# A kernel's first 30 microseconds: W_in in four equal parts behind x, halos on VectorE, a different order for W_out

## The chip, the cores and the metric

The kernel runs on one core of one Trainium2 chip. The metric is the device time of one execution in microseconds (us). A profile's own span is some 1.5 to 2 us shorter than the time of its execution, so spans are compared only with spans, and times only with times. One profile of each kernel is kept. That of the kernel before fell in a run of 683.38 us, which only one of its 34 other runs on record beats; against its span, a difference therefore comes out some 0.5 us larger than the same difference of the times. "Clock" is the mean clock that was granted to TensorE over an execution, with 1.000 as the full one.

## The reference, cut to what matters

```python
# x: (8, 4096, 192) float32; weight: (8, 7); w_in: (192, 2048); w_out: (2048, 192)
w = softmax(weight, axis=-1)                    # 8 heads, 7 taps
x_pad = concatenate([zeros((8, 6, 192)), x], axis=1)
x_unf = x_pad[:, idx, :].reshape(8, 4096, 7, 8, 24)
x = einsum('hk,bskhg->bshg', w, x_unf)          # causal convolution along s, weights shared in a head
h = x.reshape(32768, 192) @ w_in
g = 0.5 * h * (1.0 + erf(h / sqrt(2)))          # exact Gelu
out = g @ w_out
```

## The kernel before

The 32,768 tokens are worked off in blocks. A block takes `w` tokens from each of two halves of the token range, one half on partitions 0 to 63, the other on 64 to 127, and the 192 channels as three planes of 64. Blocks 0 and 1 have 256 tokens in each half, and TensorE computes their convolution with seven diagonal weight matrices (`dg`). From block 2 on VectorE computes it. Then TensorE multiplies by W_in, ScalarE takes the Gelu, and TensorE multiplies by W_out.

Everything that the change touches belongs to the start. GpSimd issues W_in, builds the identity matrix, and then does the halos of block 0 (the tokens just ahead of each strip of 32) and the casts of block 1:

```python
        @block.gpsimd
        def _(g):
            # win_in(c0, c1, sm): two transfers, one for each half of W_in's columns
            win_in(FP[0], FP[1], S_WIN[0])          # FP = [0, F/8, 2F/8, F/2]
            # ... wait for the memset, build the identity idb ...
            for i in range(1, 3):
                win_in(FP[i], FP[i + 1], S_WIN[i])  # part 2 is twice as large
            # ...
            g.wait_ge(S_IDN, 2)
            halo(0)      # zeros, then one copy a plane, each after its transpose
            halo(1)
            for p in range(NP):
                cast(g, 1, p)
            # ... casts of W_out, further halos ...
```

The queue of SP carries x and W_out. It waits once, for the first part of W_in, and the rest goes in one order:

```python
        @block.sync
        def _(sp):
            sp.dma_start(wsb[:, :], ...).then_inc(S_WSB, 16)   # the convolution's weights
            load(sp, 0, (0, 1))                     # half of block 0's x; ScalarE issues the other
            sp.wait_ge(S_WIN[0], 32)
            load(sp, 1)
            # ... four transfers of W_out, 384 KB each ...
            load(sp, 2)
            load(sp, 3)
```

VectorE prepares the weights, then transposes, copies and duplicates W_in, so that both halves of the partitions have all of it. TensorE begins with matmuls on zeros, the warm-up; in the profile of before their weight loads come 0.43 us apart up to 4.21 us, and then eight in 1.61 us:

```python
            for p in range(NP):                     # VectorE
                trans(0, p)
            conv_out(v, 0, 1)
            conv_out(v, 0, 4)
            dup(0)
            dup(1)
            for p in range(NP):
                trans(1, p)
            dup(2)
            # ...
            for i in range(16):                     # TensorE
                t.matmul(hp[1][:, 0:512], warm[:, 0:128], warm[:, :])
```

## Time and profile before

| | before |
|---|---|
| time, median of 3 | 683.76 us (683.46 to 684.16) |
| span of the profile | 681.6 us |
| TensorE busy | 675.0 us, 99% |
| first Gelu of block 0 | 10.10 us |
| transposes of block 1 | 12.41 us |
| transposes of block 2 | 19.65 us |
| first weight load of block 2 | 29.14 us |

A line of the timeline reads: start in us, how long the group was busy, engine, source line, operation, result and operands with their shapes, number of instructions, and in brackets the idle time of the engine before it and what ended it. A line of busy time by stretch has the stretch, its length, the busy time and number of instructions of TensorE's matmuls (PE), its weight loads (PEld), VectorE (DVE), ScalarE (ACT) and GpSimd (POOL), then the granted clock, the DMA share and the GB/s that the DMA engines moved. A line of waits has: who waited, for what, us in all, how often, the longest.

```profile
1.32 1.40 POOL L384 DMA_DIRECT2D win<-in_moe_w_in_dram  x2 [0.80 <-POOLq L905]
...
13.89 0.96 PE L711 MATMUL ob<-xTb,dg 64*64 64x256 bf16 x28
...
15.65 1.02 ACT L681 ACTIVATE gT<-hp 128x1024 bf16<-128x1024 f32 x1 [0.63 <-PE hp L760]
```

### The profile page before, as it was taken

The page shows a single profiled execution, that of the slowest core. Times are in us where ns is not written, and L with a number is a line of the kernel's source. Part 1 is how long each engine was busy: PE and PEld are TensorE (multiplying, and loading weights), DVE is VectorE, ACT ScalarE, POOL GpSimd, SP SyncE. Part 2 cuts the span into 40 slices and gives each one's busy share as a digit, 9 for nine tenths or more (in the row PEclk, how much of TensorE's full clock was granted, in tenths as well). Part 3 has the DMA queues.
Part 4 walks back from the last instruction along what each step waited for, and adds up shares of the span by engine and source line. Part 5 has one row for each costly group of instructions (what it writes and reads, how often), then busy time and mean ns, then how long its engine had stood idle before and what let it go on. Part 6 is the DMA issues. An engine that isn't in the chain of part 4 may idle for free.

```text
span 681.6 us, 27317 instructions
## 1 busy us (share of the span) xinstructions
PE 675.0 (99%) x12576; PEld 410.1 (60%) x12576; DVE 561.0 (82%) x904; ACT 537.3 (79%) x550; POOL 38.9 (6%) x57
## 2 busy tenths in 40 slices
PE   8999999999999999999999999999999999999998
PEld 4899655555555555555555555555555555555556
DVE  6899979888889888899888898888898888988611
ACT  6899988787787777787777788777878777878772
POOL 5026000000000000000000000000000000000000
PEclk9999999999999999999999999999999999999999
DMA  9446323234332244332244422334322434310123
GB/s 222 86 101 134 79 60 75 43 75 95 96 94 58 45 91 94 95 86 47 60 94 95 94 69 46 78 94 96 94 52 46 95 94 96 83 42 21 48 49 94
DMA packets 132994, 54.79 MB, mean 80 GB/s; under 512 B 126480, under 2 KB 132752, under 8 KB 132880
## 3 DMA queue, kind: packets, MB, share of 16 engines
q1 hardware_dynamic: 130960, 51.50, 32.5%
q8 instruction: 98, 1.61, 1.0%
q0 software_dynamic: 1248, 0.79, 0.9%
q10 hardware_dynamic: 672, 0.76, 0.4%
q14 instruction: 16, 0.13, 0.1%
HBM read 28.66 MB, written 25.17 MB: 79 GB/s over the span
## 4 chain that ended last, share of the span: by engine, by line
PE 96%; ACT 2%; DMA 1%; issue 0%; DVE 0%; SPq 0%; ACTq 0%
PE hp L760 48%; PE ob L824 43%; PE ob L791 6%; ACT gT L681 2%; DMA xin<-in_x_dram 1%; PE ob L711 0%; ACT xc L191 0%; ACT osb L269 0%; DVE osb L311 0%; DVE xT L526 0%; ACT xTb L630 0%; SPq L872 0%; DVE osb L280 0%; SPq L329 0%; ACTq L629 0%
## 5 line engine op out<-in xcount | busy, mean ns | idle before, releaser
L681 ACT ACTIVATE gT<-hp 128x1024 bf16<-128x1024 f32 x512 | 523.3, 1024 | 128.8 <-PE hp L760 125.5
L760 PE MATMUL hp<-xc,win 64*64 64x512 bf16 (+2 forms) x6048 | 419.5, 366 | 1.5 <-ACT gT L681 0.7
L824 PE MATMUL ob<-gT,wout 64*64 64x512 bf16 x5376 | 366.3, 376 | 0.0
L559 DVE SCALAR_TENSOR_TENSOR acc<-xT,wcol,acc 128x512 f32<-128x512 f32 (+1 forms) x495 | 314.1, 698 | 0.0
L760 PEld LDWEIGHTS hp<-xc,win 64*64 64x64 bf16 (+1 forms) x6048 | 189.9, 106 | 134.8 <-ACT gT L681 2.5
L824 PEld LDWEIGHTS ob<-gT,wout 64*64 64x64 bf16 x5376 | 172.3, 118 | 122.8
L311 DVE STREAM_TRANSPOSE osb<-ob 128x512 f32<-128x512 f32 x84 | 74.1, 885 | 100.8 <-PE ob L824 100.8
L526 DVE STREAM_TRANSPOSE xT<-xin 128x512 f32<-128x512 f32 (+1 forms) x105 | 78.6, 797 | 3.8 <-DMA xin<-in_x_dram 3.8
L559 DVE SCALAR_TENSOR_TENSOR xc<-xT,wcol,acc 128x512 bf16<-128x512 f32 (+1 forms) x99 | 65.0, 708 | 0.0
L447 POOL COPY xT<-xT 128x18 f32<-128x18 f32 x30 | 27.9, 930 | 505.2 <-DVE xT L526 482.9
L791 PE MATMUL ob<-wout,gT 64*128 64x192 bf16 x1024 | 52.9, 243 | 0.3
L791 PEld LDWEIGHTS ob<-wout,gT 64*128 64x128 bf16 x1024 | 44.9, 94 | 5.2 <-PE ob L791 0.6
L552 DVE TENSOR_SCALAR acc<-xT,wcol 128x512 f32<-128x512 f32 (+1 forms) x90 | 37.5, 474 | 1.1
L282 ACT ACTIVATE osb<-ob 128x192 f32<-128x192 f32 x4 | 1.3, 332 | 9.5 <-PE ob L791 9.5
L280 DVE COPY osb<-ob 128x192 f32<-128x192 f32 x4 | 1.4, 358 | 8.4 <-PE ob L791 8.4
L695 PE MATMUL hp<-warm 128*128 128x512 bf16 x16 | 5.1, 485 | 1.3 <-DVE warm L463 1.3
L269 ACT ACTIVATE osb<-ob 128x384 f32<-128x384 f32 x12 | 5.8, 486 | 0.0
L654 ACT ACTIVATE acc<-xT,wcol 128x256 f32<-128x256 f32 (+1 forms) x9 | 5.2, 575 | 0.0
L695 PEld LDWEIGHTS hp<-warm 128*128 128x128 bf16 x16 | 1.8, 119 | 4.0 <-issue 1.9
L384 POOL DMA_DIRECT2D win<-in_moe_w_in_dram x6 | 3.9, 658 | 0.8 <-POOLq L905 0.8
L711 PE MATMUL ob<-xTb,dg 64*64 64x256 bf16 (+1 forms) x112 | 3.2, 245 | 0.7 <-ACT xTb L630 0.7
L193 DVE CAST xc<-ob 64x256 bf16<-64x256 f32 (+3 forms) x8 | 2.8, 357 | 1.3 <-PE ob L711 1.1
(31 smaller groups left out, 22.4 us busy)
## 6 DMA issues: line engine op xcount, KB each, us to landing
out_dram<-osb SPq DMA_DIRECT2D x122, 192.0 KB, 3.1
xin<-in_x_dram SPq DMA_DIRECT2D x116, 192.0 KB, 4.1
xin<-in_x_dram SPq DMA_DIRECT2D x20, 96.0 KB, 4.2
woutf<-in_moe_w_out_dram SPq DMA_DIRECT2D x4, 384.0 KB, 6.2
win<-in_moe_w_in_dram POOLq DMA_DIRECT2D x4, 96.0 KB, 4.6
win<-in_moe_w_in_dram POOLq DMA_DIRECT2D x2, 192.0 KB, 5.1
out_dram<-osb SPq DMA_DIRECT2D x8, 48.0 KB, 1.9
out_dram<-osb ACTq DMA_DIRECT2D x4, 96.0 KB, 1.9
```

The lines of the kernel that those rows point to most:

```text
L269: e.activation(out=dst, in_=src, func=AF.Copy).then_inc(S_EVA)
L311: v.transpose(ap(osb[m % 2], j, [[8 * C, 128], [C // 2, TB // 32], [NP, 32]]), bank(ring(m, j)),).then_inc(S_EV)
L447: g.tensor_copy(dst, src).then_inc(S_HALO)
L526: v.transpose(ap(xT[n % 2], p * XW + HX, [[NP * XW, 128], [1, w]]), ap(xin[n % NX], p, [[TB // 32 * DQ, 128], [D if n == 0 else DQ, w // 3 ...
L552: ins = v.tensor_scalar(a, src, wk, None, ALU.mult)
L559: ins = v.scalar_tensor_tensor(dst, src, wk, a, op0=ALU.mult, op1=ALU.add)
L654: a.activation(out=acc[n % 2][:, p * TB : p * TB + w], in_=ap(xT[n % 2], p * XW + HX, [[NP * XW, 128], [1, w]]), func=AF.Copy, scale=wcol[ ...
L681: a.activation(out=ap(gT[n % 2], i * c * 2 * w, dst), in_=ap(hp[u % 2], 0, src), func=AF.Gelu,).then_inc(S_GELU)
L695: t.matmul(hp[1][:, 0:512], warm[:, 0:128], warm[:, :])
L760: ins = t.matmul(hp[u % 2][fo : fo + fw, o : o + w], ap(win, f1, [[NP * F, 64], [2, fw]]), xc[n % 2][r, p * TB : p * TB + w], start=(p == ...
L791: ins = t.matmul(bank(bb[sub], w=C), gT[m % 2][r, c0 : c0 + 128], wout[r, CH[sub][i] * C : (CH[sub][i] + 1) * C], start=(ph == 0 and i == ...
L824: ins = t.matmul(bank(ring(m, j), slice(64 * h, 64 * h + 64), w), ap(wout, 64 * hf * NF * C + CH[h][i] * C + j, [[NF * C, 64], [NP, 64]],) ...
```

## The change

The intent is to let block 0's x move without W_in beside it by making W_in wait, to shrink that x, to take GpSimd out of block 0's path, to let the duplicates of W_in follow smaller parts, and to let the first eight units of block 0's results need only half of W_out.

```diff
             def win_in(i):                        # four parts, F/8 columns of each half, 1 KB rows
-            win_in(FP[0], FP[1], S_WIN[0])        # GpSimd: first of all
-            for i in range(1, 3):
-                win_in(FP[i], FP[i + 1], S_WIN[i])
             g.wait_ge(S_IDN, 2)
             halo(0)                               # now only the zeros
+            g.wait_ge(S_PRO, 1)                   # VectorE has seen the convolution's weights land
+            for i in range(4):
+                win_in(i)
...
-                    src = [[mb * D, 32], [1, mb * D - DQ]]      # block 0's x: long rows, 720 KB
+                    src = [[mb * D, 32], [D, mb], [1, DQ]]      # 384-byte rows, 384 KB
...
             for p in range(NP):                   # VectorE
                 trans(0, p)
+                v.wait_ge(S_TR, p + 1)
+                v.tensor_copy(...).then_inc(S_HALV)             # halo, was GpSimd's
+            v.wait_ge(S_TR, NP)
+            v.tensor_copy(...).then_inc(S_CASTV)                # third cast, was ScalarE's
             conv_out(v, 0, 1)
             conv_out(v, 0, 4)
             dup(0)
             dup(1)
+            dup(2)
             for p in range(NP):
                 trans(1, p)
-            dup(2)
+            dup(3)
...
-            for i in range(16):                   # TensorE: warm-up
+            for i in range(10):
...
-            share = {1: [4, 8, 8, 8, 9, 9, 9, 9]}
+            share = {1: [4, 4, 9, 9, 9, 9, 10, 10]}   # block 0's result units behind each unit of block 1
+                if m == 0:                        # W_out's first half serves both groups first
+                    us.sort(key=lambda q: not (q[1] == 0 and q[2] < 4))
...
-            sp.wait_ge(S_WIN[0], 32)              # SP, ahead of block 1's x
+            sp.wait_ge(S_WIN[1], 32)
```

More of the change, by code (lines that the diff above doesn't have):

```diff
@@ L135, in bass_lightweight_conv__then__act_gelu_exact_kernel @@
         S_WSB = sem("S_WSB")
-        S_WIN = [sem("S_WIN%d" % i) for i in range(3)]
+        S_WIN = [sem("S_WIN%d" % i) for i in range(4)]
         S_WOUT = [sem("S_WOUT%d" % i) for i in range(4)]
@@ L148, in bass_lightweight_conv__then__act_gelu_exact_kernel @@
         S_CAST = [sem("S_CAST%d" % i) for i in range(len(PC))]
+        S_CASTV = sem("S_CASTV")
         S_PC = sem("S_PC")
@@ L153, in bass_lightweight_conv__then__act_gelu_exact_kernel @@
         S_HALO = sem("S_HALO")
+        S_HALV = sem("S_HALV")
         S_TR = sem("S_TR")
@@ L206, in bass_lightweight_conv__then__act_gelu_exact_kernel @@
         FH = F // 2
-        FP = [0, FQ, 2 * FQ, FH]
         WG = [0, 4, 2, 6]
@@ L224, in bass_lightweight_conv__then__act_gelu_exact_kernel @@
         for n in range(NB):
-            HC.append(HC[n] + (1 + NP if n == 0 else 1))
+            HC.append(HC[n] + 1)
         def wcols(hf, f):
@@ L321, in load @@
                 off = ((q // 2) * HALF + OFF[n]) * D + DQ * (q % 2)
+                dst = [[TB // 32 * DQ, 32], [DQ, mb], [1, DQ]]
                 if n == 0:
-                    dst = [[TB // 32 * DQ, 32], [1, mb * D - DQ]]
-                    src = [[mb * D, 32], [1, mb * D - DQ]]
+                    src = [[mb * D, 32], [D, mb], [1, DQ]]
                 else:
-                    dst = [[TB // 32 * DQ, 32], [DQ, mb], [1, DQ]]
                     src = [[D, 32], [32 * D, mb], [1, DQ]]
@@ L381, in _, with win_in @@
         def _(g):
-            def win_in(c0, c1, sm):
+            def win_in(i):
+                c0 = FQ * i
                 for hf in range(2):
                     g.dma_start(
-                        ap(win, 64 * hf * NP * F + c0, [[NP * F, 64], [F, NP], [1, c1 - c0]]),
-                        ap(wint, hf * FH + c0, [[NP * F, 64], [F, NP], [1, c1 - c0]]),
-                    ).then_inc(sm, 16)
-            win_in(FP[0], FP[1], S_WIN[0])
+                        ap(win, 64 * hf * NP * F + c0, [[NP * F, 64], [F, NP], [1, FQ]]),
+                        ap(wint, hf * FH + c0, [[NP * F, 64], [F, NP], [1, FQ]]),
+                    ).then_inc(S_WIN[i], 16)
             g.wait_ge(S_MSET, 1)
@@ L411, in halo @@
                     ).then_inc(S_HALO)
-                    for p in range(NP):
-                        g.wait_ge(S_TR, p + 1)
-                        g.tensor_copy(
-                            ap(t, p * XB + 1, [[NP * XB, 128], [32, HB], [1, 31]]),
-                            ap(
-                                xT[0],
-                                p * XW + HX + WS[0] - HL,
-                                [[NP * XW, 128], [32, HB], [1, 31]],
-                            ),
-                        ).then_inc(S_HALO)
                     return
@@ L504, in dup @@
                             win,
-                            64 * (1 - hf) * NP * F + FH + FP[s],
-                            [[NP * F, 64], [F, NP], [1, FP[s + 1] - FP[s]]],
-                        ),
-                        ap(
-                            win,
-                            64 * hf * NP * F + FP[s],
-                            [[NP * F, 64], [F, NP], [1, FP[s + 1] - FP[s]]],
-                        ),
+                            64 * (1 - hf) * NP * F + FH + FQ * s,
+                            [[NP * F, 64], [F, NP], [1, FQ]],
+                        ),
+                        ap(win, 64 * hf * NP * F + FQ * s, [[NP * F, 64], [F, NP], [1, FQ]]),
                     ).then_inc(S_DUPE)
@@ L525, in trans @@
                         v.wait_ge(S_HALO, HC[n])
+                    if n == 2:
+                        v.wait_ge(S_HALV, NP)
                 v.transpose(
@@ L530, in trans @@
                         p,
-                        [[TB // 32 * DQ, 128], [D if n == 0 else DQ, w // 32], [NP, 32]],
+                        [[TB // 32 * DQ, 128], [DQ, w // 32], [NP, 32]],
                     ),
@@ L581, in _ @@
                 trans(0, p)
+                v.wait_ge(S_TR, p + 1)
+                v.tensor_copy(
+                    ap(xTb[0], p * XB + 1, [[NP * XB, 128], [32, HB], [1, 31]]),
+                    ap(xT[0], p * XW + HX + WS[0] - HL, [[NP * XW, 128], [32, HB], [1, 31]]),
+                ).then_inc(S_HALV)
+            v.wait_ge(S_TR, NP)
+            v.tensor_copy(
+                ap(xTb[0], (NP - 1) * XB + HL, [[NP * XB, 128], [1, WS[0]]]),
+                ap(xT[0], (NP - 1) * XW + HX, [[NP * XW, 128], [1, WS[0]]]),
+            ).then_inc(S_CASTV)
             conv_out(v, 0, 1)
@@ L627, in _ @@
             a.wait_ge(S_PRO, 9)
-            for p in range(NP):
+            for p in range(NP - 1):
                 a.wait_ge(S_TR, p + 1)
@@ L700, in pconv @@
                 if k == KS - 1:
-                    t.wait_ge(S_CAST[PC[n]], p + 1)
+                    if n == 0 and p == NP - 1:
+                        t.wait_ge(S_CASTV, 1)
+                    else:
+                        t.wait_ge(S_CAST[PC[n]], p + 1)
                     if n == 0:
@@ L704, in pconv @@
                 if k == KS - 2:
-                    t.wait_ge(S_HALO, HC[n] + 2 + p if n == 0 else HC[n + 1])
+                    t.wait_ge(S_HALO, HC[n + 1])
+                    if n == 0:
+                        t.wait_ge(S_HALV, p + 1)
                 for hf in range(2):
@@ L743, in mm1 @@
                         t.wait_ge(S_CV, cvd(n))
-                if n == 0 and i < 3:
+                if n == 0 and i < 4:
                     t.wait_ge(S_WIN[i], 32)
-                if n == 0 and 4 <= i < 7:
+                if n == 0 and i >= 4:
                     t.wait_ge(S_DUPE, 2 * (i - 4) + 2)
@@ L844, in units @@
                     return [(ps, i) for ps in range(3) for i in range(NF)]
-                return [
-                    (g, ph, i) for g in range(NG[m]) for ph in range(2) for i in range(NF)
-                ]
+                us = [(g, ph, i) for g in range(NG[m]) for ph in range(2) for i in range(NF)]
+                if m == 0:
+                    us.sort(key=lambda q: not (q[1] == 0 and q[2] < 4))
+                return us
             for n in range(NB):
```

## The prediction

> **What bounds the kernel now.** I read the page first, then busy time by stretch, then the timeline of the first 32 us instruction by instruction, then the waits of the engines and of the DMA queue. The engine totals first:
>
> ```profile
> PE 675.0 (99%) x12576; PEld 410.1 (60%) x12576; DVE 561.0 (82%) x904; ACT 537.3 (79%) x550; POOL 38.9 (6%) x57
> ```
>
> TensorE is busy for 675.0 of 681.6 us, so only 6.6 us of its idle time exist at all. The stretches say where:
>
> ```profile
> 0.00:5.00 5.00, 3.74 (x11) 1.43 (x12) 2.42 (x13) 3.36 (x6) 3.74 (x11) 1.00 0.64 161
> 5.00:10.00 5.00, 3.94 (x77) 2.51 (x76) 3.13 (x9) 2.48 (x7) 2.18 (x7) 1.00 1.23 177
> 10.00:15.00 5.00, 4.24 (x82) 2.81 (x78) 3.34 (x7) 4.88 (x5) 1.99 (x4) 1.00 1.05 323
> 15.00:20.00 5.00, 4.73 (x104) 3.50 (x101) 3.27 (x8) 4.11 (x6) 2.95 (x5) 1.00 1.26 226
> 20.00:25.00 5.00, 4.93 (x108) 4.46 (x104) 4.96 (x15) 3.89 (x4) 0.31 (x1) 1.00 0.31 57
> 30.00:35.00 5.00, 5.00 (x113) 5.00 (x109) 4.96 (x14) 4.37 (x6) 0.31 (x1) 1.00 0.42 98
> ```
>
> (Columns: stretch, length, busy PE, PEld, DVE, ACT, POOL, clock, DMA share, GB/s.) From 30 us TensorE is full. Everything that the diff touches lies before that, so the change can only move the moment at which the full stretch begins. The first stretch also counts the warm-up matmuls as busy, which compute nothing. The timeline of that part:
>
> ```profile
> 4.62 0.63 DVE L491 TENSOR_TENSOR dg<-idb,wcol 128x448 bf16<-128x448 bf16 x1
> 5.93 1.33 DVE L526 STREAM_TRANSPOSE xT<-xin 128x256 f32<-128x256 f32 x3 [0.68 <-DMA xin<-in_x_dram]
> 6.52 1.15 POOL L414 CAST xTb<-xT 128x186 bf16<-128x186 f32 x3 [0.48 <-DVE xT L526]
> 6.55 1.17 ACT L630 ACTIVATE xTb<-xT 128x256 bf16<-128x256 f32 x3 [2.23 <-DVE xT L526]
> 7.02 1.68 PE L711 MATMUL ob<-xTb,dg 64*64 64x256 bf16 x56 [0.71 <-ACT xTb L630]
> 8.01 1.38 ACT L191 ACTIVATE xc<-ob 128x256 bf16<-128x256 f32 x4 [0.30 <-PE ob L711]
> 10.10 4.92 ACT L681 ACTIVATE gT<-hp 128x1024 bf16<-128x1024 f32 x5 [0.71 <-PE hp L760]
> ...
> 13.79 1.99 DVE L502 COPY win<-win 64x1536 bf16<-64x1536 bf16 x2
> ...
> 19.65 1.35 DVE L526 STREAM_TRANSPOSE xT<-xin 128x256 f32<-128x256 f32 x3 [1.54 <-DMA xin<-in_x_dram]
> ...
> 27.77 1.26 DVE L559 SCALAR_TENSOR_TENSOR xc<-xT,wcol,acc 128x256 bf16<-128x256 f32 x3
> ...
> 29.14 0.58 PEld L760 LDWEIGHTS hp<-xc,win 64*128 64x128 bf16 x12 [0.15 <-issue]
> ```
>
> Two paths run from start to 29.14, where block 2's first matmuls begin. **Path A**: x of block 0 lands, is transposed, cast, convolved on TensorE (7.02), copied out, multiplied by W_in, and the first Gelu starts at 10.10. From there eight Gelus of 1.02 us, with block 1's convolution matmuls wedged in, set the pace until block 1 begins at 18.01; then TensorE is full. **Path B**: x of block 2 lands only at 19.65 (VectorE idles 1.54 us for it), and from then VectorE works without a gap until the last result of block 2's convolution, 27.77 + 1.26 = 29.03. TensorE's weight load follows at 29.14 after 0.15 us of idle that the profile calls issue. The preceding weight loads ended at 28.21 + 0.78 = 28.99, so both paths arrive together, B last by about 0.15 us. A gain on A alone is worth at most that 0.15 us unless B moves too.
>
> [...]
> 1. [...] the DMA share is 1.05 to 1.26 from 5 to 20 us, while W_in (GpSimd), x and W_out (SP) are all in flight. [...]
> 2. [...] The trace's bf16 copies fit such a fixed part: 64x768 takes 0.42 us (1.77 for four), 64x1536 takes 0.68, so 0.16 us is left at zero size.
> 3. [...] Here warm-up weight loads come 0.43 us apart up to 4.21 us, then eight in 1.61 us[...].
> 4. [...] This trace shows contention between compute instructions (a GpSimd cast took 0.65 beside a VectorE copy against 0.40 alone; a copy 1.28 against 0.68), but not that W_in's issue suffers from it.
>
> **The change part by part.**
> *x of block 0.* Four loads of 180 KB in long rows become four of 96 KB in 384-byte rows: 720 to 384 KB, and W_in now waits until wsb has landed, so it no longer shares the engines with x. Last landing now is 5.93 minus a few hundredths. With the same issue times (0.88 to 2.05 us) and the quickest landing of such a line at 2.5 us, I estimate 4.5 to 5.0. But VectorE's own program has dg before the transpose, until 4.62 + 0.63 = 5.25. So the transposes start at 5.27, gaining 0.66 and not 1.2 us.
> *Halos and the third cast on VectorE.* GpSimd took 0.38 us a halo, beside the transposes. [...] Each halo also waits for its own transpose (about 0.04 us). Chain from 5.27: transpose to 5.79, halo 6.08, transpose to 6.52, halo 6.81, transpose to 7.25, halo 7.54, cast 7.79. ACT's cast of plane 1 ends at 6.52 + 0.10 + 0.42 = 7.04 (before 7.31), but plane 2 is ready at 7.79 (before 7.72). The 0.66 us is eaten by the serial chain. Convolution starts at 6.36 instead of 7.02, but planes 1 and 2 finish within 0.05 us of before, and ACT's four copies from 8.4 us on then lead to the first Gelu at about 10.03: gain 0.07 us.
> *Ten warm-up matmuls for sixteen.* They end near 4.9 us; [...] Zero.
> *W_in.* Eight issues of 0.63 us (six took 3.93), started at about 2.4 us after the reduce at 2.17, end at 7.6. Parts then land[...] near 6, 7, 8.3 and 9.5 us. Each is wanted at 8.9, 9.9, 11.2 and 12.1 by TensorE, so none delays it. The SP queue now waits for part 1, about 6.9, where it waited for part 0 and resumed at 6.53: block 1's x and W_out are issued 0.4 us later, but meet less W_in, because x's traffic shrank by 336 KB and W_in is no longer queued deep ahead of them.
> *The duplicate copies.* The pair of 0.68 and 1.28 us after block 1's transposes becomes a pair of 0.42 before and a pair after. VectorE is free for block 1's copies at about 14.5, not 15.78; the sixth unit's matmuls (16.06) come about 0.1 us earlier, and Gelu 7 follows. Gain 0.13 us.
> *W_out's order.* The first eight of 64 result units need only half of W_out, whose last cast runs at 18.22 to 19.05. No wait on it is seen now in TensorE's idle, so this is insurance for an earlier start. Work is unchanged: 0.
> *Sum.* Path A: 0.07 + 0.13 = 0.2 us. Path B: block 2's x lands by my estimate about 1 us earlier, since the same queue carries less[...]. Then B has slack and the start of block 2 follows A: the 0.15 us of waiting goes as well. Total 0.35 us: 683.76 - 0.35 = 683.4.
>
> **The rivals.**
> *R1: block 2's x lands later.* SP waits for a later part of W_in; if GpSimd's first bytes take 2.5 us after issue (they came in the packets of before only as x's were ending), part 1 lands at 8 us, everything behind it moves by up to 1.5 us, and path B ends at 29.6 to 30.2. The time becomes 684.4 to 685. For it: B has no slack. Against: x is out of W_in's way.
> *R2: VectorE's serial chain is longer,* [...] With 0.15 us on each of four instructions the first Gelu moves to 10.6: about 684.1. [...]
> *R3: the gain of x passes through whole* (0.66 us, because ACT, not the copies of planes 1 and 2, sets the Gelu) and B moves too: 682.9.
>
> **Range and chances.** The sum gives 683.4. R3 and run-to-run spread (683.46 to 684.16) give the low side, 682.6; R1 and R2 give the high side, 684.4. I put 0.25 on R1 or R2. A change of 2% is 13.7 us, twice all TensorE's idle time, so faster is nearly excluded[...].
>
> **What would show it.** In the timeline after: transposes of block 0 directly behind dg at 5.25 (first step); halo copies of 0.25 us, cast ready near 7.8; convolution at 6.4 with a hole in it; first Gelu near 10.0; block 2's transposes near 18.7 and VectorE done before TensorE needs it at about 28.9. If the transposes of block 2 start after 19.65, R1 holds; if the halos take over 0.35 us, R2; if the first Gelu is before 9.6, R3. A cold clock (warm-up weight loads still 0.43 us apart at the end and slow convolution matmuls) would break the prediction altogether.

(The sum came to 0.35 us, hence 683.4: 0.07 and 0.13 us on path A, and 0.15 us of waiting once path B has slack. The 0.07 comes from the chain of VectorE; for a halo and for the third cast the profile after measured 0.26 and 0.29 us, and 0.03 to 0.04 us from a transpose's end to its halo. The zero for the ten warm-ups rested on a limit for idle time, and the landings of W_in's parts on an allowance after their last issue; neither was shown. Path B's 1 us was the estimate, and no working from measured numbers stands for it.)

## More of the kernel before

```profile
SPq L329 <- DMA win<-in_moe_w_in_dram: 4.5, 1, 4.5
```

GpSimd issues W_in's first part at 1.32 us; block 1's convolution runs at 13.89 us without having waited; the sixth Gelu starts at 15.65.

## The result, and the profile after

The changed kernel took 685.79 us in the median of four runs (684.94 to 687.52); the kernel before, on the same chip in the same rounds, took 683.96 (683.46 to 684.24). The ratio is 1.0031, with a 95% interval of 1.0007 to 1.0054. It is thus slightly slower, well within 2%, and above the predicted range. (All ratios here are the mean time of one kernel's fast runs over that of the other's of the same rounds, so not quite the ratio of the quoted medians.) The four runs fall into two pairs: 684.94 and 684.97 at a clock of 1.000, and 686.61 and 687.52 at 0.998 and 0.997. The profiled run is the 686.61.

The engine totals of the changed kernel, from its page:

```profile
PE 676.4 (99%) x12570; PEld 407.7 (60%) x12570; DVE 561.9 (82%) x910; ACT 537.3 (78%) x549; POOL 38.5 (6%) x56
```

TensorE's busy time grew by 1.4 us with six matmuls fewer; so some of them ran more slowly. Busy time by stretch, changed kernel:

```profile
0.00:5.00 5.00, 3.74 (x9) 1.34 (x10) 2.41 (x13) 3.37 (x6) 3.22 (x11) 1.00 0.46 93
5.00:10.00 5.00, 4.00 (x76) 2.27 (x76) 4.18 (x13) 2.23 (x7) 2.98 (x6) 1.00 1.16 142
10.00:15.00 5.00, 3.02 (x46) 1.74 (x42) 2.24 (x6) 4.83 (x5) 0.12 (x1) 1.00 0.99 285
15.00:20.00 5.00, 4.56 (x80) 3.00 (x82) 3.26 (x9) 1.02 (x1) 4.08 (x7) 0.66 1.17 253
20.00:25.00 5.00, 4.53 (x94) 3.92 (x90) 4.27 (x13) 4.71 (x5) 0.86 (x3) 1.00 0.46 100
```

Three things differ from before. The DMA engines move 93 and 142 GB/s in the first two stretches, where it was 161 and 177. TensorE is busy for 3.02 us from 10 to 15 us instead of 4.24. And from 15 to 20 us the granted clock is 0.66, where it was 1.00 throughout.

The timeline of the changed kernel:

```profile
2.63 5.14 POOL L385 DMA_DIRECT2D win<-in_moe_w_in_dram  x8 [0.51 <-DVE wmx L458]
...
5.17 0.51 DVE L515 STREAM_TRANSPOSE xT<-xin 128x256 f32<-128x256 f32 x1
5.72 0.26 DVE L573 CAST xTb<-xT 128x186 bf16<-128x186 f32 x1
...
6.25 2.34 PE L717 MATMUL ob<-xTb,dg 64*64 64x256 bf16 x56 [0.54 <-ACT xTb L631]
...
9.92 4.93 ACT L682 ACTIVATE gT<-hp 128x1024 bf16<-128x1024 f32 x5 [0.71 <-PE hp L766]
...
14.30 1.32 DVE L515 STREAM_TRANSPOSE xT<-xin 128x256 f32<-128x256 f32 x3 [2.66 <-DMA xin<-in_x_dram]
...
15.34 1.78 PE L717 MATMUL ob<-xTb,dg 64*64 64x256 bf16 x28 [1.55 <-POOL xTb L214]
...
17.05 1.46 PE L766 MATMUL hp<-xc,win 64*128 64x256 bf16 x12
...
18.55 1.02 ACT L682 ACTIVATE gT<-hp 128x1024 bf16<-128x1024 f32 x1 [3.70 <-PE hp L766]
...
21.03 1.34 DVE L515 STREAM_TRANSPOSE xT<-xin 128x256 f32<-128x256 f32 x3 [0.66 <-DMA xin<-in_x_dram]
...
29.14 1.27 DVE L548 SCALAR_TENSOR_TENSOR xc<-xT,wcol,acc 128x256 bf16<-128x256 f32 x3
```

Read it in two halves. Up to 9.92 us everything is as intended: block 0's transposes start 0.76 us earlier, and the first Gelu 0.18 us earlier. After that both later blocks are late. Block 1's x lets its transposes start at 14.30 instead of 12.41 us; TensorE waits 1.55 us for it, and Gelu, which follows, idles 3.70 us. Block 2's x starts its transposes at 21.03 instead of 19.65, and VectorE's chain ends at 29.14 + 1.27 = 30.41 instead of 29.03.

The wait of SP's queue for W_in, changed kernel:

```profile
SPq L328 <- DMA win<-in_moe_w_in_dram: 5.2, 1, 5.2
```

It ends at 7.86 us in the chain of waits, where the queue of before resumed at 6.53.

In this profile block 2's first weight load is at 32.29 us, 3.15 us later than before, and the span grew by 684.8 - 681.6 = 3.2 us. VectorE's chain accounts for 1.4 of them. The other 1.8 belong to TensorE, which was still behind with block 1. The matmuls at 17.05 show why: twelve take 1.46 us, and twelve of the same form took 0.83 at 12.95 us, where the granted clock was 1.00. In stretches of half a microsecond the granted clock is 0.50 from 16.1 to 19.5 us: half of 3.4 us, so by estimate 1.7 us of TensorE's work, are lost there.

### The profile page after: what moved, and what is told of

Read it like the earlier page. It is cut to its first block, busy times and chain, and to the rows that moved or that the text cites. A ratio compares the mean times of both kernels' runs of the same rounds, so it can differ in the third digit from the quotient of the medians.

```text
span 684.8 us, 27315 instructions
## 1 busy us (share of the span) xinstructions
PE 676.4 (99%) x12570; PEld 407.7 (60%) x12570; DVE 561.9 (82%) x910; ACT 537.3 (78%) x549; POOL 38.5 (6%) x56
## 3 DMA queue, kind: packets, MB, share of 16 engines
q8 instruction: 98, 1.61, 1.0%
## 4 chain that ended last, share of the span: by engine, by line
PE 95%; ACT 2%; DMA 1%; POOL 0%; issue 0%; DVE 0%; SPq 0%
PE hp L766 47%; PE ob L830 42%; PE ob L797 5%; ACT gT L682 1%; DMA xin<-in_x_dram 1%; DMA win<-in_moe_w_in_dram 0%; PE ob L717 0%; POOL win L385 0%; DMA wsb<-in_weight_dram 0%; SPq L328 0%; ACT osb L270 0%; DVE osb L312 0%; POOL xTb L214 0%; DVE xT L515 0%; DVE osb L281 0%
## 5 line engine op out<-in xcount | busy, mean ns | idle before, releaser
L766 PEld LDWEIGHTS hp<-xc,win 64*64 64x64 bf16 (+1 forms) x6048 | 187.9, 106 | 136.7 <-ACT gT L682 2.9
L717 PE MATMUL ob<-xTb,dg 64*64 64x256 bf16 (+1 forms) x112 | 4.8, 288 | 2.4 <-POOL xTb L214 1.6
L717 PEld LDWEIGHTS ob<-xTb,dg 64*64 64x64 bf16 x112 | 3.2, 124 | 4.7 <-POOL xTb L214 2.1
```

The lines of the kernel that those rows point to most:

```text
L717: ins = t.matmul(bank(kd, slice(64 * ho, 64 * ho + 64), w), dg[r, d0 : d0 + 64], xTb[PC[n]][r, x0 : x0 + w], start=(k == KS - 1), stop=(k ...
L766: ins = t.matmul(hp[u % 2][fo : fo + fw, o : o + w], ap(win, f1, [[NP * F, 64], [2, fw]]), xc[n % 2][r, p * TB : p * TB + w], start=(p == ...
```

## The experiments

The theories, when the experiments began:

- **G, the gate.** SP's queue waits for W_in's second part instead of the first, so block 1's x, W_out and block 2's x are issued late.
- **W, W_in's start.** W_in's first transfer is issued 1.3 us later (2.63 against 1.32). What isn't moved in that time is missing later, and all that is queued behind comes late.
- **P, the parts.** Four parts of 1 KB rows move more slowly than three.
- **C, the clock.** The wait at 15 us makes the clock drop, and that is the whole loss.
- **Rest.** The VectorE halos, the duplicates or W_out's order cost time.

(The texts name the theories in their own words or letters; the numbers beside them say which reading is meant. S there is W here, and R is P, except in the prediction, where R1 to R3 are its rivals.) In what follows "block 2 at" is the start of block 2's transposes.

### The changed kernel once more (e1)

No edit. It runs beside the next three, to have its spread and a second profile.

> The changed kernel as it is, for its spread. Theory G (SP's gate on W_in's second part delays block 1's x, so TensorE waits for its casts): times of about 685.0 us where the clock stays at 1.000, because that wait is in every run. Theory C [...]: in some of the runs about 2 us more, 686.6 to 687.5, with a granted clock of 0.997 to 0.998. If all runs are at 685.0 with clock 1.000, C is an accident of one session; if the spread is even and not in two groups, C is wrong.

Measured: 685.41 us (685.01 to 686.56), ratio 1.0024 (1.0011 to 1.0036). One of five runs had a clock below 1.000 (686.56 at 0.997). The profile fell in a run at full clock; from its timeline:

```profile
6.42 3.11 PE L717 MATMUL ob<-xTb,dg 64*64 64x256 bf16 x56 [0.71 <-ACT xTb L631]
...
10.91 4.92 ACT L682 ACTIVATE gT<-hp 128x1024 bf16<-128x1024 f32 x5 [1.07 <-PE hp L766]
...
21.25 1.34 DVE L515 STREAM_TRANSPOSE xT<-xin 128x256 f32<-128x256 f32 x3 [2.66 <-DMA xin<-in_x_dram]
```

Block 2's x is late again (21.25) and VectorE waits 2.66 us for it, in a run without a clock dip; the span is 683.3, or 1.7 above the profile of before, some 0.5 of which is that profile's quick run. So there is a loss with the late x and without a dip, and C isn't the whole of it. Over both sets of runs, the six of the changed kernel at clock 1.000 average 685.2, or 1.2 above the 684.0 of the kernel before, and the three below it 686.9: where the dip comes, it goes with another 1.7 us, the 1.7 worked out above. (The groups are not always this clear: e6 and e9 below each have a run of 686.19 at clock 1.000.)

The first line has something else. The 56 matmuls of block 0's convolution take 3.11 us instead of 2.34, and the first Gelu comes at 10.91 instead of 9.92: after ten warm-ups it ran slowly in this run. The warm-ups themselves don't tell the two profiles apart: their weight loads come 0.43 us apart to the end in both. Nor does the clock column: it reads 1.00 up to 10 us in both. Of the eight profiles with ten warm-ups, the convolution is fast (2.34 to 2.37 us) in the four in which it begins by 6.36 us and slow (3.11) in the four in which it begins at 6.42 or later.

### The gate back to W_in's first part (e2), and the gate alone in the kernel before (e3)

```diff
 # e2, on the changed kernel            # e3, on the kernel before
-sp.wait_ge(S_WIN[1], 32)               -sp.wait_ge(S_WIN[0], 32)
+sp.wait_ge(S_WIN[0], 32)               +sp.wait_ge(S_WIN[1], 32)
```

> The changed kernel, but SP waits for W_in's part 0, as before, ahead of block 1's x. Theory G: SP resumes near 6.4 us instead of 7.86, block 1's x lands near 12.5 instead of 14.3, TensorE's wait for the casts goes (under 0.3 us), the clock stays at 1.000 in all runs, and the time is 683.3 to 683.9, no slower than the kernel before. Rival W (W_in itself, issued from 2.6 us on and in eight pieces, fills the engines until 11.5 us whatever SP does): x still lands at 13.5 or later, and the time stays at 684.7 to 685.2. Rival F (the instruction fetch of 16 KB at 11.9 us holds up one DMA engine): the last share of x lands over 1 us behind the others again and the time is 684.5 or more.

> The kernel before, with only SP's gate moved to W_in's part 1, which landed at 8.7 us there against 6.5 of part 0. Theory G: block 1's x is issued about 2.2 us later and lands near 14 us; the first matmuls of its convolution move from 13.9 to 15 or later, and the time rises by 1 to 2 us to 684.7 to 686, with some runs at a lower clock. Rival W: W_in is as it was, so x lands at 12.4 to 13 and the time stays within 0.4 us of before.

e2: 685.5 us (684.27 to 685.88), ratio 1.0020 (1.0007 to 1.0032). SP resumed at 6.34, earlier than in the kernel before, and yet block 1's transposes started at 13.79 and block 2's at 20.93:

```profile
20.93 1.35 DVE L515 STREAM_TRANSPOSE xT<-xin 128x256 f32<-128x256 f32 x3 [1.09 <-DMA xin<-in_x_dram]
```

What changed places is in TensorE's waits:

```profile
PE hp L766 <- DMA win<-in_moe_w_in_dram: 1.7, 1, 1.7
```

Now it is W_in's last part that is late: TensorE waits 1.7 us for it and begins its matmuls at 13.52. Undoing the gate only moved the wait, and G falls as the cause of what the change costs. (The fetch that rival F names is in the changed kernel's trace, 16 KB at 11.87 us; that it holds up an engine wasn't shown.)

e3: 684.66 us (684.03 to 685.53), ratio 1.0011 (0.9998 to 1.0023), block 2 at 20.52, span 682.5. In the kernel before, the later gate alone delays block 2 by 0.87 us; the time follows by about 0.7, at the edge of what the interval tells apart. Block 1 started at 12.95, short of the 14 that the text expected of G. So the gate can hurt, but taking it away isn't enough.

### Keeping TensorE busy across the wait (e4)

```diff
                     mm1(n, i)
+                    if (n, i) == (0, 4):
+                        for _ in range(6):
+                            t.matmul(bank(3), warm[:, 0:128], warm[:, :])
```

> The changed kernel with six dummy matmuls of 512 columns (1.3 us at full clock, results overwritten) between the fifth unit's matmuls and block 1's convolution, that is, inside TensorE's wait for the casts. Theory C [...]: no run under clock 1.000, all runs in one group near 684.9 to 685.2. Rival (the clock dips for another reason, or the short warm-up is the cause): still some runs 2 us longer with clock 0.997 to 0.998.

(For the 1.3 us of six such matmuls: the later warm-ups of before, of the same 512 columns, have eight weight loads in 1.61 us, 0.2 each.)

Measured: 685.26 us (684.5 to 685.78), ratio 1.0017 (1.0004 to 1.0031), clock 1.000 in all five runs, block 2 at 21.28, span 683.5. No dip in five runs fits the reading that idleness causes it, but with one dip in e1's five runs it doesn't prove it. The late x stays, and so does the loss: C is at most an addition.

### W_in without its wait (e5), and in three parts (e6)

```diff
 # e5, on the changed kernel            # e6, on the changed kernel
-            g.wait_ge(S_PRO, 1)        -            for i in range(4):
             for i in range(4):         +            for i in range(3):   # parts 2 and 3 joined, 2 KB rows
                 win_in(i)                               win_in(i)
```

> The changed kernel without GpSimd's wait for the first reduce, so W_in's eight issues start near 2.2 instead of 2.6 us and end near 7.3 instead of 7.8. Theory S (W_in starts too late, so all that is queued after it is late): W_in's last part and block 2's x land 0.4 to 0.5 us earlier (x near 20.7 instead of 21.2) and the time falls by as much, to 684.6 to 685.0. Theory R (1 KB rows[...]): little changes, 685.0 to 685.4.

> The changed kernel with W_in's third and fourth part joined to one of 2 KB rows as before (six issues for eight), still back to back after the wait. Theory R: issues end near 6.5 instead of 7.8 us, W_in has landed by 10.3, block 2's x lands near 20.0 and the time falls to 683.8 to 684.3. Theory S: x of block 2 still lands at 20.9 or later, time 684.9 to 685.5.

e5: 685.39 us (684.97 to 686.59), ratio 1.0024 (1.0011 to 1.0036). W_in's first issue moved only from 2.63 to 1.99 us, since it still stands behind the identity and the zeros. Block 0's x now landed later (transposes at 5.91), the first Gelu came at 11.23, and block 2 at 21.64. This run shows what the wait was for. It missed what W expected (block 2's x near 20.7, 684.6 to 685.0 us): half of the 1.3 us came back, and block 2 was not earlier. With narrow rows of x beside W_in an earlier W_in did not help here, and W has to stand on e7 and e13.

e6: 685.08 us (684.39 to 686.19), ratio 1.0020 (1.0006 to 1.0033), block 2 at 21.34. Its rate from 5 to 10 us is 146 GB/s. P falls in this direction.

### W_in as before in the changed kernel (e7), four parts in the kernel before (e8)

```diff
 # e7, on the changed kernel: issue order, parts and gate of before; narrow x and ten warm-ups stay
+            win_in(0)                  # first of all
             # ... identity ...
+            for i in range(1, 3):
+                win_in(i)
-            g.wait_ge(S_PRO, 1)
-            for i in range(4):
-                win_in(i)
-            sp.wait_ge(S_WIN[1], 32)
+            sp.wait_ge(S_WIN[0], 32)
 # e8, on the kernel before
-        FP = [0, FQ, 2 * FQ, FH]
+        FP = [0, FQ, 2 * FQ, 3 * FQ, FH]
```

> The changed kernel with W_in as before in all: part 0 first of all, three parts, SP waiting for part 0; left of the change are x's narrow rows, the halos and third cast on VectorE, the shorter warm-up, the split duplicates and W_out's order. If W_in is the whole cause (R or S or both): block 2's x lands at 19.3 to 19.8, the first Gelu is at 9.9 to 10.1, no gap before block 1's convolution over 0.3 us, and the time is 683.5 to 684.0, as before or 0.3 us better. If it stays at 684.8 or more, the cause is x's narrow rows or VectorE's part.

> The kernel before with only W_in's last part split in two of 1 KB rows (part 0 still first of all, so it starts as early as before). Theory R: W_in ends later, block 2's x lands at 20.2 to 20.8 instead of 19.6, and the time rises by 0.6 to 1.2 us, to 684.6 to 685.2. Theory S: within 0.3 us of before. GpSimd's halos wait about 0.6 us for the longer issue, which delays the first Gelu to about 10.6 in both theories but not block 2's x.

e7: 685.24 us (684.84 to 685.94), ratio 1.0022 (1.0010 to 1.0035). The timeline says that the one thing was mended and another broken:

```profile
6.76 0.52 DVE L517 STREAM_TRANSPOSE xT<-xin 128x256 f32<-128x256 f32 x1 [1.51 <-DMA xin<-in_x_dram]
...
7.84 3.11 PE L719 MATMUL ob<-xTb,dg 64*64 64x256 bf16 x56 [2.51 <-ACT xTb L633]
...
19.42 1.34 DVE L517 STREAM_TRANSPOSE xT<-xin 128x256 f32<-128x256 f32 x3 [0.18 <-DMA xin<-in_x_dram]
```

With W_in early, block 2 is on time (19.42, even before the 19.65 of the kernel before), which is what W demands. But block 0's x in 384-byte rows is now beside W_in and lands at least 1.6 us later than in the changed kernel (6.76 against 5.17, where it was VectorE's own work that set the start), while the long rows of before were ready at 5.93 in the same company. TensorE has nothing from the end of ten warm-ups to 7.84, its convolution takes 3.11 us (in this profile the granted clock averages 0.82 from 5 to 10 us and 0.84 from 10 to 15), and the first Gelu is at 12.16. Path A is now the late one: VectorE is done at 28.81, TensorE begins block 2 only 2.2 us after that, at 31.01, and the span is 683.5 all the same. The time missed the 683.5 to 684.0 that the text gave for W_in as the whole cause. So the two halves of the change hang together: narrow rows need W_in to wait, and W_in's wait makes block 2 late.

e8: 684.11 us (683.82 to 684.40), ratio 1.0004 (0.9991 to 1.0016), block 2 at 20.13, span 682.7. Four parts of 1 KB rows in the kernel before cost 0.3 us by the medians, which the interval doesn't tell from nothing. P's 0.6 to 1.2 us did not come; it falls from this side too.

### Sixteen warm-ups (e9)

```diff
-            for i in range(10):
+            for i in range(16):
```

> The changed kernel with sixteen warm-up matmuls as before instead of ten. Theory H ([...]in two profiles of the changed form its 56 matmuls took 3.1 us against 2.3): in every profile the convolution takes about 2.3 us and the first Gelu starts 3.7 us after its first matmul (9.9 to 10.1 us, or somewhat later if the warm-up itself runs past 6.3). The time falls only a little, to 684.6 to 685.2, because block 2's x (21 us) still sets the end. If the convolution is still slow in the profile, the number of warm-ups isn't the cause.

(The 56 matmuls in this text are those of block 0's convolution; H is that ten warm-ups are the reason why it is slow in some profiles.)

Measured, on the changed kernel: 685.88 us (684.93 to 686.60), ratio 1.0028 (1.0016 to 1.0040). The profile has the first Gelu at 9.92, the convolution in 2.34 us, and block 2 at 21.19 with a span of 683.2. Compare with e1, whose first Gelu came a whole microsecond later: its span is 683.3. A gain of 1 us on path A was worth 0.1 us, since path B ends last. The median missed the expected 684.6 to 685.2, and one of the five runs had a clock of 0.998 (686.60), so sixteen warm-ups don't keep the dip away either. The short warm-up is then not what the changed kernel loses by.

### Block 2's x made late on purpose (e10), and block 1's (e11)

```diff
 # e10, on the kernel before            # e11, on the kernel before
-            load(sp, 2)                -            load(sp, 1)
             load(sp, 3)                             for i in range(4):
+            load(sp, 2)                +                if i == 1:
                                        +                    load(sp, 1)
```

> The kernel before with one swap in SP's queue: block 3's x ahead of block 2's. Nothing else moves: W_in, block 1's x, W_out and all of TensorE's work up to block 2 stay. Theory B (block 2's x, through VectorE's convolution, sets when TensorE enters the full stretch, with 0.15 us or less of slack): block 2's x lands about 1.5 to 2 us later (21.1 to 21.6), VectorE ends block 2 at 30.5 to 31.0 and the time rises by the same 1.4 to 1.9 us, to 685.2 to 685.8. Rival (only block 1's x and the Gelu chain matter): time within 0.4 us of before.

> The kernel before with block 1's x behind the first quarter of W_out in SP's queue: block 1's x about 1 us later, W_out's first quarter as much earlier, block 2's x unmoved. Theory A (block 1's x is just in time for its convolution, which stands in TensorE's order between block 0's units): its convolution starts at 14.8 to 15.2 instead of 13.9, TensorE waits about 1 us for GpSimd's casts, and the time rises by 0.7 to 1.1 us, to 684.5 to 685.0; some runs may be more if the clock closes in the wait. Rival: within 0.3 us of before.

e10 only swaps two loads, and what it makes late is block 2's x alone:

```profile
20.97 1.34 DVE L526 STREAM_TRANSPOSE xT<-xin 128x256 f32<-128x256 f32 x3 [2.84 <-DMA xin<-in_x_dram]
...
29.08 1.27 DVE L559 SCALAR_TENSOR_TENSOR xc<-xT,wcol,acc 128x256 bf16<-128x256 f32 x3
```

Block 1 starts at 12.44 as before, block 2 1.32 us later, and the span is 682.9, or 1.3 us longer. The time is 684.81 us (684.40 to 685.09), ratio 1.0015 (1.0003 to 1.0027), against 683.82. TensorE's weight loads stand idle for 0.86 us before block 2. This is the shown link: a later block 2 goes through to the end, one for one between these two profiles, and with 1.0 us in the times.

e11: 685.79 us (684.22 to 687.52), ratio 1.0029 (1.0014 to 1.0044). Block 1's transposes moved to 15.27, and the waits of TensorE have

```profile
PE ob L711 <- POOL xTb L213: 1.7, 1, 1.7
```

Three of its six runs had a clock of 0.997 or 0.998 (686.69, 686.76, 687.52), the others 1.000 (684.22, 684.37, 684.88). In the profiled one, the 687.52, the granted clock averages 0.74 from 15 to 20 us and 0.92 from 20 to 25. Two groups like those of the changed kernel are thus made in the kernel before by nothing but a late block 1's x (W_out's first quarter, which passes it, comes earlier). So the wait for block 1's x is enough to bring the dip; the shorter warm-up, which e11 doesn't have, isn't needed for it.

### Everything but W_in, x's rows and the warm-up (e12)

The kernel before with the halos and the third cast on VectorE, the duplicates split in four, and W_out's order:

```diff
             for p in range(NP):
                 trans(0, p)
+                v.wait_ge(S_TR, p + 1)
+                v.tensor_copy(...).then_inc(S_HALV)
+            v.tensor_copy(...).then_inc(S_CASTV)
...
+            dup(2)
             for p in range(NP):
                 trans(1, p)
-            dup(2)
+            dup(3)
...
+                    us.sort(key=lambda q: not (q[1] == 0 and q[2] < 4))
```

> What is left of the change when W_in, x of block 0 and the warm-up are as before: halos and third cast on VectorE, split duplicates, W_out's first half first. Block 2's x at 19.4 to 19.8 as before. The prediction's working for VectorE's chain applied to transposes from 5.93: third cast at 8.45 instead of 7.72, first Gelu at 10.6 to 10.7 instead of 10.1; less 0.1 us for the duplicates: time 684.1 to 684.5. If it is 683.8 or less, VectorE's chain costs nothing; if over 684.8, one of these parts hides a cost of its own.

Measured: 683.86 us (683.80 to 683.93), ratio 1.0001 (0.9989 to 1.0014).

```profile
19.76 1.35 DVE L519 STREAM_TRANSPOSE xT<-xin 128x256 f32<-128x256 f32 x3 [1.94 <-DMA xin<-in_x_dram]
```

The first Gelu is at 10.73, as the text expected of VectorE's longer chain, but the time didn't rise to its 684.1. Taken together these parts cost nothing and gain nothing in the time. What the change costs lies in W_in's issue, x's rows and the warm-up.

### W_in held, and nothing else (e13)

```diff
-            win_in(FP[0], FP[1], S_WIN[0])
             # ... identity, zeros of the halo ...
-            for i in range(1, 3):
-                win_in(FP[i], FP[i + 1], S_WIN[i])
+                    g.wait_ge(S_PRO, 1)
+                    for i in range(3):
+                        win_in(FP[i], FP[i + 1], S_WIN[i])
```

> The kernel before with only this: GpSimd makes its identity and the halo's zeros first and then waits for the first reduce before it issues W_in, as in the changed kernel; three parts, x's wide rows and all else as before. Theory S (the 1.3 us that W_in's issue loses at the start, when the DMA engines have room, is missing later, as the queue never catches up): the engines move 140 to 155 GB/s in 5 to 10 us instead of 177, block 2's x lands at 20.6 to 21.2 and the time rises by 0.8 to 1.5 us, to 684.6 to 685.3. Rival (the late start costs nothing with wide rows of x, the narrow rows are needed for the loss): block 2's x at 19.5 to 20.0 and time within 0.3 us of before.

On the kernel before, with its long rows, three parts, first gate and sixteen warm-ups. From its timeline, and one line of its busy time by stretch:

```profile
2.64 3.89 POOL L384 DMA_DIRECT2D win<-in_moe_w_in_dram  x6 [0.52 <-DVE wmx L466]
...
21.17 1.35 DVE L525 STREAM_TRANSPOSE xT<-xin 128x256 f32<-128x256 f32 x3 [1.75 <-DMA xin<-in_x_dram]
...
29.30 1.26 DVE L558 SCALAR_TENSOR_TENSOR xc<-xT,wcol,acc 128x256 bf16<-128x256 f32 x3
```

```profile
5.00:10.00 5.00, 4.34 (x70) 2.18 (x70) 2.81 (x8) 2.48 (x7) 2.71 (x7) 1.00 1.13 140
```

This single edit brings all marks of the changed kernel: 140 GB/s (142), block 1's transposes at 13.73 (13.93 in e1), block 2's at 21.17 (21.25), span 683.1 (683.3). The time is 684.71 us (684.44 to 684.89), ratio 1.0012 (0.9998 to 1.0027), against 683.77. The interval of the time just includes no change; but three of the four runs are slower than all 12 of before, and the fourth is slower than 11 of them. The gate is not what carries the delay: SP's queue resumed at 6.74 us, and in e12, whose block 2 is on time, at 6.76. Up to 20 us the engines moved 0.23 MB less than before (841 against 887 GB/s times 5 us), with the same bytes to move. The shortfall is not in the first 5 us (154 against 161), where x's long rows move, but in the next five (140 against 177). So W stands as far as this: the late issue of W_in alone is enough to make block 2 late. By which way wasn't shown: by the packets in the traces W_in began to move at 4.48 us in the profile of before and at 4.19 in that of the changed kernel, and its last packet ended at 10.32 and 11.10.

### Long rows in the changed kernel (e16), another gate (e14, e15)

```diff
 # e16, on the changed kernel
-                    src = [[mb * D, 32], [D, mb], [1, DQ]]
+                    src = [[mb * D, 32], [1, mb * D - DQ]]
 # e15, on the kernel before; e14, on e12
-            sp.wait_ge(S_WIN[0], 32)
+            sp.wait_ge(S_XIN[0], 64)
```

> The changed kernel with block 0's x in its wide rows as before (720 KB instead of 384 KB); W_in late and in four parts. Theory S: block 2's x still lands at 20.8 or later and the time stays at 685.0 to 686. If the narrow rows were the cause, x of block 2 comes at 19.8 or earlier and the time at 684.3 or less. In both, the transposes of block 0 start at 5.9 instead of 5.2, so the first Gelu comes at 10.6 or later.

> The parts of the change that cost nothing (halos and cast on VectorE, split duplicates, W_out's first half first; W_in, x's rows and warm-up as before) with the same earlier gate on block 0's x. VectorE is done with the duplicates 1 us earlier than in the kernel before, and block 2's x lands near 19.3: time 683.4 to 683.9, at best 0.4 us under before. If over 684.2, the earlier gate takes bandwidth from W_in that the Gelu chain needs.

> The kernel before with SP waiting for block 0's x (5.9 us) instead of W_in's part 0 (6.5 us) ahead of block 1's x. From the two gates of the kernel before (6.53 gives 19.64 for block 2's x, 7.72 gives 20.52: 0.74 us per us) block 2's x lands 0.4 us earlier, at 19.2; the time falls by what path A leaves, 0.15 us, to 683.5 to 683.8. If W_in's part 1 gets late by the sharing and a Gelu waits for it, the time rises by up to 0.5 us.

e16: 684.80 us (684.72 to 685.33), ratio 1.0017 (1.0004 to 1.0030), block 2 at 21.55. Long rows don't bring block 2 back. All four runs had a clock of 0.997 or 0.998; in the profile the clock is at 0.50 from 7.7 to 11.1 us, after TensorE had waited 2.00 us for block 0's x, which was ready at 6.00.

e15 (683.75 us, 683.41 to 684.37, ratio 1.0001, block 2 at 19.95) and e14 (684.26 us, 683.81 to 685.21, ratio 1.0005, block 2 at 21.45) looked for a better version: no wait on W_in in SP's queue at all, only on block 0's x. Neither beats the kernel before. e14 is also a warning: its W_in is early and its rate from 5 to 10 us is 168 GB/s, and still its profiled run had a late block 2. That run was the slowest of the four (685.21, the others 683.81 to 684.37), and its engines moved still less by 20 us than those of e13 (831 against 841 GB/s times 5 us). Why is open. It shows that a late W_in is not the only way to a late block 2, and, as the other three runs are 0.8 to 1.4 us quicker, that single profiles of one kernel may differ by such amounts.

### The profiles beside each other

| kernel | W_in's first issue | GB/s, 5 to 10 us | block 1 at | block 2 at | span |
|---|---|---|---|---|---|
| before | 1.32 | 177 | 12.41 | 19.65 | 681.6 |
| e12 rest of the change | 1.32 | 197 | 12.48 | 19.76 | 682.1 |
| e15 before, other gate | 1.32 | 176 | 13.20 | 19.95 | 682.2 |
| e8 before, four parts | 1.32 | 176 | 13.12 | 20.13 | 682.7 |
| e3 before, later gate | 1.32 | 195 | 12.95 | 20.52 | 682.5 |
| e10 before, loads swapped | 1.32 | 196 | 12.44 | 20.97 | 682.9 |
| e14 rest, other gate | 1.31 | 168 | 13.79 | 21.45 | 683.4 |
| e13 before, W_in held | 2.64 | 140 | 13.73 | 21.17 | 683.1 |
| e9 changed, 16 warm-ups | 2.63 | 151 | 13.89 | 21.19 | 683.2 |
| e1 changed | 2.80 | 142 | 13.93 | 21.25 | 683.3 |
| e4 changed, filler | 2.63 | 133 | 14.45 | 21.28 | 683.5 |
| e6 changed, three parts | 2.75 | 146 | 13.88 | 21.34 | 683.4 |
| e16 changed, long rows | 2.63 | 144 | 13.80 | 21.55 | 683.6 |
| e5 changed, no wait | 1.99 | 143 | 13.17 | 21.64 | 683.7 |

From e3 downwards the span less the start of block 2 is 661.9 to 662.2 us, and it is 661.95 in the kernel before: where path B ends last, the span simply follows it. (e4, at the upper end, has TensorE a little behind as well.) e12, e15 and e8 have 662.3 to 662.6; in these path A is the later one: block 2's first weight load follows the end of VectorE's chain by 0.4 to 0.6 us, against 0.1 where B is last. Left out are the runs in which a dip or a late start of the convolution (7.84 us in e7) made TensorE late: after and e2 (dip, spans 684.8 and 684.2), e7 and e11.

How much of the delay is the missing traffic? Up to 20 us the four stretches of before add up to 887 GB/s times 5 us, or 4.44 MB, and those of the changed kernel to 773, or 3.87 MB. Of the 0.57 MB of difference, 0.34 are the 336 KB by which block 0's x shrank. The remaining 0.23 MB are late, and at the 253 GB/s of that last stretch take 0.9 us. This is an estimate; 1.4 us were measured in that profile. (e13 lacks the same 0.23 MB, with x unshrunk.) The order of the transfers counts too: e3 and e10 moved 195 and 196 GB/s from 5 to 10 us, more than the 177 of before, and had block 2 at 20.52 and 20.97. No run splits the rest exactly.

The profiles also show a pattern in the clock dips. In five of the eighteen TensorE's matmuls had a wait of 1.55 us or more after the warm-up: the changed kernel (1.55), e11 (1.66), e2 (1.69), e16 (2.00) and e7 (2.51). In each of the five the granted clock was then at 0.50 for 3.4 us, beginning 0.2 to 1.1 us after the wait ended. In the other thirteen, whose longest wait up to 30 us was 0.47 to 1.28 us, the clock reads 1.00 in every stretch up to 25 us. This fits idleness as the cause; it is a pattern of single profiles and no tested limit. Nor does every dip cost time: e7's three runs at 0.998 (684.84 to 685.24) are quicker than its two at 1.000 (685.86 and 685.94).

## Why the prediction was wrong, point by point

The step that failed is the third: block 2's x was to come 1 us earlier and came some 1.5 us later, and path B, which ends last, took that to the end. It accounts for the runs at full clock, 684.9 to 685.6. The unforeseen clock dip adds about 1.7 us in the others, and the median of 685.79 lies between the two groups.

- **Where the time is set: right.** Two paths, B last by 0.15 us, a gain on A worth nothing unless B moves. e9 and e10 confirm both directions. The 0.15 us belong to one profile: in e8, e12 and e15, whose block 2 is nearly on time, A ends last by a few tenths.
- **Block 0's chain: right.** Transposes at 5.17 (5.27 predicted), halos 0.26 us (0.25), each 0.03 to 0.04 us after its transpose (0.04), cast 0.29 us and done at 7.62 (7.79), convolution at 6.25 with a hole in it (6.36), first Gelu at 9.92 (10.03). It bought nothing, as the prediction's own reasoning demands for path A. The match is partly luck: e1, the same kernel, has its first Gelu at 10.91. The 10.10 of before is a lucky one too: in the ten profiles with sixteen warm-ups their weight loads keep the distance of 0.43 us until 4.2 us (before) or as late as 7.2, and where it is late the warm-ups hold up the convolution (e10, first Gelu at 10.74).
- **"Block 2's x lands by my estimate about 1 us earlier, since the same queue carries less": this step failed.** It started VectorE at 21.03 and 21.25 instead of 19.65, some 1.5 us later. The estimate had counted the bytes that x saves, from a rule that no trace gives, and not the 1.3 us by which W_in is issued later. e13, with exactly the bytes of before, shows that this alone brings the delay. (The prediction also has W_in in flight until 20 us; its last part had landed at 10.70 in the profile of before.)
- **"Parts then land ... near 6, 7, 8.3 and 9.5 us": failed.** They landed at 6.36, 7.84, 9.29 and 11.47 in the profile; the issue itself went as predicted (8 issues of 96 KB, 5.14 us, so 0.64 each, to 7.77). The allowance from the end of a part's last issue to its landing, which no trace gives, was too short: it took 2.3, 2.5, 2.8 and 3.7 us, and in the profile of before 3.8, 4.1 and 4.9. Why it grows from part to part no run shows.
- **SP "0.4 us later": mis-sized.** It resumed at 7.86 (8.80 in e1) instead of 6.53, so 1.3 to 2.3 us.
- **Block 1's x: missed.** The prediction saw a gain of 0.13 us from the duplicates there. The x landed up to 1.9 us later, and TensorE waited for it.
- **"Ten warm-up matmuls for sixteen ... Zero": not shown, nearly right for the time.** It rested on a limit for idle time that no trace gives. In e1 the convolution took 3.11 us instead of 2.34, and Gelu came 1 us later; path B hid it. The spacing of 0.43 us ends at 4.21 us in the profile of before, where the trace's records of the granted clock begin too (at 4.18; ahead of the first record the clock column reads 1.00), but in other profiles it lasts until 7.2; no run shows what ends it. The sign that the text gave for a cold clock, loads 0.43 us apart to the end and a slow convolution, came in e1, whose span of 683.3 is that of e9 (683.2) without it. The clock dip that does show in the time can come without any short warm-up, from the wait for block 1's x (e11).
- **R1: the right rival, for another reason.** It gave 684.4 to 685, and the runs at clock 1.000 are at 684.9 to 685.6. It named SP's gate and the late first bytes of W_in, and its 8 us for the second part was nearly met (7.84); e2 shows that the gate isn't needed for the loss, e13 that the later issue is enough. The chance of 0.25 on R1 or R2 was too small: B had no slack, so any delay of block 2's x had to show (e10: 1.32 us later, 1.0 us in the times). R2 and R3 fell: the halos took 0.26 us each, and the first Gelu wasn't before 9.6.

What stays open: the exact share of the missing traffic in the 1.5 us; whether idleness alone causes the dip (e4 had none in five runs, too few to prove it, and the pattern of the waits is only a pattern); by which way W_in's later issue makes block 2 late; and e14's late block 2.

## What to carry to other kernels

When a stretch waits for transfers, ask of each change when each of them is issued, not only how many bytes it has: here a transfer held back by 1.3 us to make room for another one made the blocks queued behind it late by about as much (1.3 and 1.5 us in e13's profile). Before you shorten a path, look at which one ends last and with what slack; here 0.15 us of slack meant that 1 us gained on the other path was worth 0.1. And run each part of a change alone: three of its parts were neutral together, one cost the time, and another (the narrow rows) was good only as long as that one stayed.
